# One wide matmul in place of two narrow ones in the output stage of a fused attention and mixture kernel

## The chip, the cores and the metric

The kernel runs on one core of one Trainium2 chip. The metric is the device time of the core in microseconds. A core has a matrix engine, TensorE (PE in the profile, its weight loads shown as PEld), the elementwise engines VectorE (DVE), ScalarE (ACT) and GpSimd (POOL), and DMA queues, here issued from SyncE (SP). PE writes its results to PSUM, which this kernel uses as eight banks of 128 x 512 words of 32 bits; ACT and DVE read them there, and POOL works on tiles in SBUF, the main on-chip memory. Each engine takes its instructions in the order in which the program has them, and waits on semaphores for the others.

## The reference, cut to what matters

```
kv  = einsum('bhsd,bhde->...')        # linear attention, 8 batches x 8 heads, 576 x 64
x   = rms-normalised q @ kv, scaled   # becomes 4608 tokens x 512
x   = P(h) / Q(h) @ w_out, h = x @ w_in           # 512 -> 2048 -> 512, P and Q polynomials
out = (silu(x @ w_gate) * (x @ w_val)) @ w_o2     # 512 -> 1536 -> 512
```

All is in float32. The part that counts here is the last product, a matrix g of 4608 x 1536 (the gated activations) times w_o2 of 1536 x 512.

## The kernel before, in words

The kernel goes through attention and the first mixture layer, then the gate and value products of the second layer, and ends with the output stage. Most matmuls take words of the type float32r (fp32r in the profile), and each of their operands is cut into a high and a low half by `split`: ACT copies the high half (line 95), and DVE or POOL subtracts it from the value to get the low half (line 98). A product of two such operands is three matmuls: high by high, high by low, low by high.

The output stage runs over 18 units: nine tiles of 512 tokens by two halves of 256 tokens (`units`, line 839). Each unit is one 2x2 block product in the Strassen-Winograd form, with seven products O_A11, O_A12, O_A22, O_S2, O_S1, O_S3 and O_S4 instead of eight. Each product (`o_product`, line 941) goes over the six slices of the inner dimension and does three matmuls for each (lines 946, 947, 948): the stationary operand is the half x of the activations, 128x128, loaded anew for each matmul, the moving one is 256 columns (HK) of the weights `wo`. One product fills half a PSUM bank, so a unit uses half of each of four banks; two sets of four banks alternate.

Other engines prepare and finish:

- `o_load` (SP) fetches g of a unit two units ahead. `o_sums_1` and `o_sums_2` (DVE, line 515, 128x768, tile graw) form the four sums of a unit. `o_split` makes the two halves of the operand of one product (ACT high, then DVE or POOL low, 128x768, tile xo). POOL makes those for A11 and A12, DVE the five others.
- Bank 0 collects three products one after the other. `o_snap` (ACT) copies it out after each: a after A11, b after S2, c after S3. PE may add the next product to the bank only after the copy.
- `o_merge` (DVE, line 515, tile sb) adds or subtracts another bank: a += bank 1; d = c - bank 2; c += bank 3; b += bank 3. Bank 3 first holds S1; after d and c are merged, S4 is added to it, and then it is merged into b. So PE's product S4 of a unit waits for that unit's merge c.
- `o_store` (SP) writes the unit out.

The order is written out by hand in `o_unit` (line 967). PE's order in unit v is A11, A12, S4 of unit v-1, A22, S2, S1, S3. DVE's is: merge d and merge c of unit v-1, splits S1 and S3, merge a, merge b of unit v-1, split S4, split A22 of unit v+1, four sums of unit v+1, split S2 of unit v+1. POOL's is split A11 of unit v+1, split A12 of unit v+1. In unit 1 its own split S2 stands behind the merges as well, since unit 0 does not make it. In unit 0 the products and merges of the last gate step are interleaved. The last unit (`o_last`, line 1011) has the order A11, S4 of unit 16, S2, S1, S3, S4, A22, A12, with the merges and three stores between. The weight halves `wo` are made in `o_halves` (line 889) from tiles tagged crg and crv, under the gate products.

Of the kernel before, what the change touches and what calls it, by code (L numbers as in the profile page):

```python
# [8 lines left out]
F32 = mybir.dt.float32  # L9
F32R = mybir.dt.float32r  # L10
# [3 lines left out]
ALU = mybir.AluOpType  # L14

P = 128
# [4 lines left out]
N = 512  # L21
# [20 lines left out]
def fused_kernel(ctx: ExitStack, tc: tile.TileContext, kv_main, kv_left, q_t, w_in, w_out, w_gate, w_val, w_o2, ab, g_norm, out):  # L42
# [13 lines left out]
    nc = tc.nc  # L56
# [16 lines left out]
    late = {}  # L73
# [20 lines left out]
    def act(out, in_, func=AF.Copy, **kw):  # L94
        nc.scalar.activation(out=out, in_=in_, func=func, **kw)  # L95

    def sub(eng, out, a, b):
        eng.tensor_tensor(out=out, in0=a, in1=b.bitcast(F32), op=ALU.subtract)  # L98
# [69 lines left out]
    for f in range(NF1):  # L168
        n = len(wa_src)
# [63 lines left out]
    for t in range(TILES):  # L233
        t0, ss = t * N, []
        while t0 < (t + 1) * N:
            b = t0 // S
            n = min((b + 1) * S, (t + 1) * N) - t0
# [276 lines left out]
    def tt(eng, out, a, b, op):  # L514
        eng.tensor_tensor(out=out, in0=a, in1=b, op=op)  # L515

    def halves_of(ap):
        return ap.rearrange("p (a n) -> p a n", a=2)


    HK = DM // 2
# [152 lines left out]
    steps = [(q, f) for q in range(1, len(seq)) for f in range(UP if q >= P2 else 0, NF2 if q >= P2 else UP)]  # L674
# [4 lines left out]
    def new_set(y):  # L679
        if y:  # L680
            return [ps_y.tile([P, N], F32, tag=f"y{m}", name="pb") for m in range(4)]
        b = [ps_a.tile([P, N], F32, tag=f"pa{m}", name="pb") for m in range(2)]
        return b + [ps_h.tile([P, N], F32, tag="ph", name="pb") for m in range(2)]

    def banks(i):
        if i not in bank:
            bank[i] = new_set(i % 2 == 0)
        return bank[i]
# [76 lines left out]
    def last_product(i):  # L765
        if i >= 0:
            product(i, 3, S_4, B_22, False)
# [62 lines left out]
    wo = {}  # L830
# [3 lines left out]
    o_x = {}  # L834
    o_sb = {}
# [3 lines left out]
    units = [(t, c) for t in order for c in range(2)]  # L839
    O_A11, O_A12, O_A22, O_S2, O_S1, O_S3, O_S4 = range(7)  # L840
    PRODUCTS = (V_11, V_21, V_T4, V_T2, V_T1, V_T3, V_22)
# [26 lines left out]
    def o_views(i):  # L868
        vals = [halves_of(w_views(raw_o[i, k])[2]) for k in range(2)]
        sums = [halves_of(raw_o[i, k].bitcast(F32).rearrange("p (n two) -> p n two", two=2)[:, :, 0]) for k in range(2)]  # L870
        return vals, sums
# [13 lines left out]
    def o_slot(k, shape, name):  # L885
        pool, tag = o_slots[k]
        return pool.tile(shape, F32R, tag=tag, name=name)

    def o_halves(i, part, eng):
        if part == 0:  # L890
            if i == UP - 1:
                wo[i] = [o_slot(7 + k, [P, 7, HK], "wo") for k in range(2)]
            else:
                u = late[f"u{i}"].tile([P, 2, 7, HK], F32R, tag=f"u{i}", name="wo")
                wo[i] = [u[:, k] for k in range(2)]
        vals, sums = o_views(i)
        src, at = ((vals[0][:, 0:1, :], slice(V_11, V_11 + 1)), (vals[1], slice(V_21, V_22 + 1)), (sums[0], slice(V_T1, V_T2 + 1)), (sums[1], slice(V_T3, V_T4 + 1)))[part]
        hi, lo = (w[:, at, :] for w in wo[i])
        act(hi, src)
        sub(eng, lo, src, hi)  # L900

    def o_load(v, k):
        if v < len(units):
            t, c = units[v]
            r = o_raw[v, k] = o_sum_to[v, k] = late["graw"].tile([P, UP, NH], F32, tag=f"g{k}", name="graw")
            nc.sync.dma_start(out=r, in_=g_dram[t, k][c])

    def o_part(v, k):
        a, b = T_OF[k]
        return (o_raw if k in (O_A11, O_A12, O_A22, O_A21) else o_sum_to)[v, a][:, :, b * P:b * P + P]  # L910
# [5 lines left out]
    def o_split(v, k, eng):  # L916
        if v < len(units):
            x = o_x[v, k] = o_slot(k, [P, 2, UP, P], "xo")
            r = o_part(v, k)
            act(x[:, 0], r)  # L920
            sub(eng, x[:, 1], r, x[:, 0])
# [8 lines left out]
    def o_sums_1(v):  # L930
        o_sum(v, O_S1, O_A21, O_A22, ALU.add)
        o_sum(v, O_S3, O_A11, O_A21, ALU.subtract)
# [2 lines left out]
        o_sum(v, O_S2, O_S1, O_A11, ALU.subtract)  # L935
        o_sum(v, O_S4, O_A12, O_S2, ALU.subtract)

    def o_banks(v):
        return [b[:, :HK] for b in banks(len(steps) + v)]

    def o_product(v, k, b, first=True):
        ps, x = o_banks(v)[b], o_x[v, k]
        for n, i in enumerate(I_ORDER):
            wh, wl = (w[:, PRODUCTS[k], :] for w in wo[i])
            start, stop = first and n == 0, n == UP - 1
            nc.tensor.matmul(ps, lhsT=x[:, 0, i, :], rhs=wh, start=start, stop=False, skip_group_check=not first)  # L946
            nc.tensor.matmul(ps, lhsT=x[:, 0, i, :], rhs=wl, start=False, stop=False, skip_group_check=not first)  # L947
            nc.tensor.matmul(ps, lhsT=x[:, 1, i, :], rhs=wh, start=False, stop=stop, skip_group_check=not first)  # L948

    def o_dst(v, name):  # L950
        row, col = {"a": (0, 0), "b": (0, HK), "d": (1, 0), "c": (1, HK)}[name]
        return o_sb[v][:, row, col:col + HK]

    def o_snap(v, name):
        if name == "a":
            o_sb[v] = late["p"].tile([P, 2, N], F32, tag="g", bufs=2, name="sb")
        act(o_dst(v, name), o_banks(v)[0])

    def o_merge(v, out, name, b, op=ALU.add):
        tt(nc.vector, o_dst(v, out), o_dst(v, name), o_banks(v)[b], op)  # L960

    def o_store(v, rows, cols=slice(0, N)):
        t, c = units[v]
        o = out[t * N + c * NH:t * N + c * NH + NH, :].rearrange("(m p) n -> p m n", p=P)
        nc.sync.dma_start(out=o[:, rows, cols], in_=o_sb[v][:, rows, cols])

    def o_unit(v):
        L = len(steps) - 1
        o_product(v, O_A11, 0)
        if v:  # L970
            o_merge(v - 1, "d", "c", 2, ALU.subtract)
            o_merge(v - 1, "c", "c", 3)
            if v == 1:
                o_split(v, O_S2, nc.vector)
        else:
            post(L, 0)
            o_split(v, O_S2, nc.vector)
        o_split(v, O_S1, nc.vector)
        o_split(v, O_S3, nc.vector)
        o_load(v + 2, 0)  # L980
        o_product(v, O_A12, 1)
        o_snap(v, "a")
        if v:
            o_product(v - 1, O_S4, 3, False)
        else:
            post(L, 2)
            post(L, 3)
            last_product(L)
        o_merge(v, "a", "a", 1)
        o_split(v + 1, O_A11, nc.gpsimd)  # L990
        if v:
            o_merge(v - 1, "b", "b", 3)
            o_store(v - 1, slice(0, 2))
        else:
            post(L, 4)
        o_product(v, O_A22, 2)
        o_split(v, O_S4, nc.vector)
        o_load(v + 2, 1)
        o_split(v + 1, O_A12, nc.gpsimd)
        o_product(v, O_S2, 0, False)  # L1000
        o_split(v + 1, O_A22, nc.vector)
        o_sums_1(v + 1)
        o_snap(v, "b")
        o_product(v, O_S1, 3)
        o_sums_2(v + 1)
        if v:
            o_split(v + 1, O_S2, nc.vector)
        o_product(v, O_S3, 0, False)
        o_snap(v, "c")

    def o_last(v):
        o_product(v, O_A11, 0)
        o_merge(v - 1, "d", "c", 2, ALU.subtract)
        o_merge(v - 1, "c", "c", 3)
        o_split(v, O_S1, nc.vector)
        o_split(v, O_S3, nc.vector)
        o_snap(v, "a")
        o_product(v - 1, O_S4, 3, False)
        o_product(v, O_S2, 0, False)
        o_snap(v, "b")  # L1020
        o_split(v, O_S4, nc.vector)
        o_merge(v - 1, "b", "b", 3)
        o_store(v - 1, slice(0, 2))
        o_product(v, O_S1, 3)
        o_merge(v, "b", "b", 3)
        o_product(v, O_S3, 0, False)
        o_snap(v, "c")
        o_product(v, O_S4, 1)
        o_merge(v, "b", "b", 1)
        o_store(v, slice(0, 1), slice(HK, N))  # L1030
        o_product(v, O_A22, 2)
        o_merge(v, "d", "c", 2, ALU.subtract)
        o_merge(v, "c", "c", 3)
        o_store(v, slice(1, 2))
        o_product(v, O_A12, 1)
        o_merge(v, "a", "a", 1)
        o_store(v, slice(0, 1), slice(0, HK))

    with tc.manual_schedule():
# [166 lines left out]
        for s in range(S1):  # L1206
            t, f = divmod(s, NF1)
# [61 lines left out]
            if t == TILES - 1:  # L1269
# [12 lines left out]
                elif 8 <= f < 12:  # L1282
                    k, c = divmod(f - 8, 2)
# [82 lines left out]
        for j in range(UP):  # L1366
            f, n = UP + j, 12 + 10 * j
# [19 lines left out]
        for n, i in enumerate(made):  # L1387
            at = (
# [3 lines left out]
            )[n % 3]  # L1392
# [37 lines left out]
        for v in range(len(units) - 1):  # L1430
            o_unit(v)
        o_last(len(units) - 1)


# [46 lines left out]
```

## Time and profile before

| | |
|---|---|
| time, median of 3 runs | 1680.99 us (1679.74 to 1682.69) |
| span of the profiled execution, first to last instruction | 1678.3 us (its own time is not listed) |
| PE busy | 1666.0 us, 99% of the span |
| PEld (weight loads) busy | 1415.8 us, 84% |
| DVE, ACT, POOL busy | 1371.2, 1073.6, 473.1 us |
| granted TensorE clock | 0.9 or more of full speed in all 40 slices, mean 1.000 |
| output stage | 1401.4 to 1674.9 us |

Busy PE is time in which at least one matmul runs; matmuls overlap, so the distance between the starts of two is what one costs. A group's mean is the duration of one instruction, waits for operands before it not counted. Rows of a timeline give the start, the duration (of all, where xN is over 1), the engine, the line, the tiles as out<-in with partitions x elements, and in brackets the idle time before and what ended it.

### The profile page before, as it was taken

The numbers are of one execution on the slowest core, as the hardware profiler recorded it, in microseconds if no ns is written. First come the engines' busy times: TensorE is split into PE (matmuls) and PEld (weight loads), VectorE is DVE, ScalarE is ACT, GpSimd is POOL, SyncE is SP. The second block draws the span as 40 slices with busy tenths as digits, with TensorE's granted clock in tenths as the row PEclk, the third lists the DMA queues.
The fourth block names the chain that finished last, engine by engine and source line by source line (L and its number), as shares of the span: only waits on it lengthen the run. The fifth ranks groups of instructions, "written<-read, shape, count | busy, mean of one in ns | idle before, by whom it ended". The sixth has DMA issues, their size and how long they took to land.

```text
span 1678.3 us, 24096 instructions
## 1 busy us (share of the span) xinstructions
PE 1666.0 (99%) x9040; PEld 1415.8 (84%) x9040; DVE 1371.2 (82%) x1913; ACT 1073.6 (64%) x1801; POOL 473.1 (28%) x331
## 2 busy tenths in 40 slices
PE   8999999999999999999999999999999999999999
PEld 5777888888888888888888888888888889999999
DVE  7999999999999999998996766778568859776665
ACT  7898888788788787877775444445435455444442
POOL 2112333333333343333330112223202155222221
PEclk9999999999999999999999999999999999999999
DMA  8861011011111110111425237243494354434431
GB/s 338 319 240 50 8 51 63 26 57 44 57 39 69 45 63 20 45 57 63 151 75 182 82 107 281 64 144 107 152 334 151 130 176 144 164 133 151 151 129 61
DMA packets 77850, 198.18 MB, mean 118 GB/s; under 512 B 6947, under 2 KB 35876, under 8 KB 75044
## 3 DMA queue, kind: packets, MB, share of 16 engines
q1 hardware_dynamic: 77732, 196.64, 33.3%
q8 instruction: 71, 1.16, 0.3%
q14 instruction: 47, 0.39, 0.1%
HBM read 130.02 MB, written 66.06 MB: 117 GB/s over the span
## 4 chain that ended last, share of the span: by engine, by line
PE 92%; DVE 4%; ACT 2%; DMA 2%; issue 1%; POOL 0%; SPq 0%; DVEq 0%; POOLq 0%; ACTq 0%
PE pb L112 10%; PE pb L113 10%; PE pb L114 10%; PE y L113 7%; PE ph L113 7%; PE ph L114 7%; PE ph L112 7%; PE y L114 7%; PE y L112 7%; PE pb L948 5%; PE pb L947 5%; PE pb L946 5%; DVE e L108 1%; ACT e L95 1%; DMA wraw<-in_w_in 1%
## 5 line engine op out<-in xcount | busy, mean ns | idle before, releaser
L98 POOL TENSOR_TENSOR ghl<-e,ghl 128x512 fp32r<-128x512 f32 x141 | 183.3, 1300 | 499.4 <-ACT ghl L95 289.8
L112 PE MATMUL pb<-xc,wu 128*128 128x512 f32 (+1 forms) x804 | 303.9, 378 | 0.0
L113 PE MATMUL pb<-xc,wu 128*128 128x512 f32 (+1 forms) x804 | 303.8, 378 | 0.0
L114 PE MATMUL pb<-xc,wu 128*128 128x512 f32 (+1 forms) x804 | 303.8, 378 | 0.0
L95 ACT ACTIVATE e<-pb 128x512 f32<-128x512 f32 (+1 forms) x162 | 92.8, 573 | 238.0 <-PE pb L114 237.7
L108 DVE SCALAR_TENSOR_TENSOR e<-e,e 128x512 f32<-128x512 f32 x285 | 226.3, 794 | 12.0 <-ACT e L95 4.9
L515 DVE TENSOR_TENSOR e<-e,pb 128x512 f32<-128x512 f32 (+1 forms) x216 | 140.6, 655 | 114.4 <-PE pb L114 63.5
L112 PE MATMUL ph<-x,wt 128*128 128x512 f32 x576 | 226.5, 393 | 0.3 <-ACT x L95 0.3
L113 PE MATMUL ph<-x,wt 128*128 128x512 f32 x576 | 225.0, 391 | 1.8 <-POOL x L98 1.6
L114 PE MATMUL ph<-x,wt 128*128 128x512 f32 x576 | 224.7, 390 | 0.0
L113 PE MATMUL y<-ghl,wt 128*128 128x512 f32 x564 | 221.5, 393 | 3.0 <-POOL ghl L98 2.8
L112 PE MATMUL y<-ghl,wt 128*128 128x512 f32 x564 | 221.5, 393 | 0.0
L114 PE MATMUL y<-ghl,wt 128*128 128x512 f32 x564 | 219.9, 390 | 0.0
L947 PE MATMUL pb<-wo,xo 128*128 128x256 f32 x756 | 213.9, 283 | 0.0
L948 PE MATMUL pb<-wo,xo 128*128 128x256 f32 x756 | 213.9, 283 | 0.0
L946 PE MATMUL pb<-wo,xo 128*128 128x256 f32 x756 | 213.9, 283 | 0.0
L112 PEld LDWEIGHTS pb<-xc,wu 128*128 128x128 f32 x804 | 151.0, 188 | 28.6 <-ACT e L95 0.4
L114 PEld LDWEIGHTS pb<-xc,wu 128*128 128x128 f32 x804 | 151.0, 188 | 28.1
L113 PEld LDWEIGHTS pb<-xc,wu 128*128 128x128 f32 x804 | 151.0, 188 | 28.0
L95 ACT ACTIVATE xo<-graw 128x768 fp32r<-128x768 f32 x122 | 99.1, 840 | 109.3 <-issue 49.9
L95 ACT ACTIVATE e<-ph 128x512 f32<-128x512 f32 x144 | 85.8, 596 | 119.3 <-PE ph L114 118.4
L946 PEld LDWEIGHTS pb<-wo,xo 128*128 128x128 f32 x756 | 145.1, 192 | 0.1
(138 smaller groups left out, 3409.2 us busy)
## 6 DMA issues: line engine op xcount, KB each, us to landing
graw<-gd SPq DMA_DIRECT2D x36, 768.0 KB, 4.4
gd<-gout SPq DMA_DIRECT2D x96, 256.0 KB, 2.2
kvm<-in_kv_main SPq DMA_DIRECT2D x32, 512.0 KB, 7.1
yraw<-yd SPq DMA_DIRECT2D x22, 512.0 KB, 7.0
q<-in_q_t SPq DMA_DIRECT2D x36, 256.0 KB, 3.7
yd<-sb SPq DMA_DIRECT2D x18, 512.0 KB, 3.5
out<-sb SPq DMA_DIRECT2D x17, 512.0 KB, 3.0
wraw<-in_w_in SPq DMA_DIRECT2D x16, 512.0 KB, 4.3
```

Source lines behind the costliest of these rows:

```text
L95: nc.scalar.activation(out=out, in_=in_, func=func, **kw)
L98: eng.tensor_tensor(out=out, in0=a, in1=b.bitcast(F32), op=ALU.subtract)
L108: nc.vector.scalar_tensor_tensor(out=out, in0=in0, scalar=scalar, in1=in1, op0=op0, op1=op1)
L112: nc.tensor.matmul(ps, lhsT=wh, rhs=xh, start=first, stop=False, skip_group_check=more)
L113: nc.tensor.matmul(ps, lhsT=wh, rhs=xl, start=False, stop=False, skip_group_check=more)
L114: nc.tensor.matmul(ps, lhsT=wl, rhs=xh, start=False, stop=last, skip_group_check=more)
L515: eng.tensor_tensor(out=out, in0=a, in1=b, op=op)
L946: nc.tensor.matmul(ps, lhsT=x[:, 0, i, :], rhs=wh, start=start, stop=False, skip_group_check=not first)
L947: nc.tensor.matmul(ps, lhsT=x[:, 0, i, :], rhs=wl, start=False, stop=False, skip_group_check=not first)
L948: nc.tensor.matmul(ps, lhsT=x[:, 1, i, :], rhs=wh, start=False, stop=stop, skip_group_check=not first)
```

## The change

In the 17 units before the last, the weight halves lie side by side (the high half's 256 columns, then the low half's), and the two matmuls whose stationary operand is the high half of x become one matmul of 512 columns. Its first 256 result columns hold high by high, the others high by low. The third matmul, low by high, is added to the second half of the bank. The bank is then 512 wide, and so are the snaps and merges, which write to a new tile `ob` (`o_both`, one for each row of the block, in the buffers tagged crg and crv). `o_fold` (POOL) adds the two halves at the end and writes sb; fold 1 stands behind merge c, fold 0 behind merge b, each ahead of POOL's next split in the program's order. The store then waits for the fold. The last unit keeps the three narrow matmuls. The weight tile changes its layout from [2, 7, 256] to [7, 2, 256], that of the last slice lies in two slots of four and three.

```diff
--- before.py
+++ after.py
@@ -889,13 +889,15 @@
     def o_halves(i, part, eng):
         if part == 0:
             if i == UP - 1:
-                wo[i] = [o_slot(7 + k, [P, 7, HK], "wo") for k in range(2)]
+                wo[i] = [o_slot(7 + k, [P, 4, 2, HK], "wo") for k in range(2)]
             else:
-                u = late[f"u{i}"].tile([P, 2, 7, HK], F32R, tag=f"u{i}", name="wo")
-                wo[i] = [u[:, k] for k in range(2)]
+                u = late[f"u{i}"].tile([P, 7, 2, HK], F32R, tag=f"u{i}", name="wo")
+                wo[i] = [u[:, 0:4], u[:, 4:7]]
         vals, sums = o_views(i)
         src, at = ((vals[0][:, 0:1, :], slice(V_11, V_11 + 1)), (vals[1], slice(V_21, V_22 + 1)), (sums[0], slice(V_T1, V_T2 + 1)), (sums[1], slice(V_T3, V_T4 + 1)))[part]
-        hi, lo = (w[:, at, :] for w in wo[i])
+        k = at.start // 4
+        w = wo[i][k][:, at.start - 4 * k:at.stop - 4 * k]
+        hi, lo = w[:, :, 0, :], w[:, :, 1, :]
         act(hi, src)
         sub(eng, lo, src, hi)
 
@@ -935,29 +937,46 @@
         o_sum(v, O_S2, O_S1, O_A11, ALU.subtract)
         o_sum(v, O_S4, O_A12, O_S2, ALU.subtract)
 
-    def o_banks(v):
-        return [b[:, :HK] for b in banks(len(steps) + v)]
+    def o_bank(v, b):
+        ps = banks(len(steps) + v)[b]
+        return ps if v < len(units) - 1 else ps[:, :HK]
 
     def o_product(v, k, b, first=True):
-        ps, x = o_banks(v)[b], o_x[v, k]
+        ps, x = o_bank(v, b), o_x[v, k]
         for n, i in enumerate(I_ORDER):
-            wh, wl = (w[:, PRODUCTS[k], :] for w in wo[i])
+            w = wo[i][PRODUCTS[k] // 4][:, PRODUCTS[k] % 4]
             start, stop = first and n == 0, n == UP - 1
-            nc.tensor.matmul(ps, lhsT=x[:, 0, i, :], rhs=wh, start=start, stop=False, skip_group_check=not first)
-            nc.tensor.matmul(ps, lhsT=x[:, 0, i, :], rhs=wl, start=False, stop=False, skip_group_check=not first)
-            nc.tensor.matmul(ps, lhsT=x[:, 1, i, :], rhs=wh, start=False, stop=stop, skip_group_check=not first)
+            if v < len(units) - 1:
+                nc.tensor.matmul(ps, lhsT=x[:, 0, i, :], rhs=w, start=start, stop=stop, skip_group_check=not first)
+                nc.tensor.matmul(ps[:, HK:], lhsT=x[:, 1, i, :], rhs=w[:, 0, :], start=False, stop=stop, skip_group_check=True)
+            else:
+                nc.tensor.matmul(ps, lhsT=x[:, 0, i, :], rhs=w[:, 0, :], start=start, stop=False, skip_group_check=not first)
+                nc.tensor.matmul(ps, lhsT=x[:, 0, i, :], rhs=w[:, 1, :], start=False, stop=False, skip_group_check=not first)
+                nc.tensor.matmul(ps, lhsT=x[:, 1, i, :], rhs=w[:, 0, :], start=False, stop=stop, skip_group_check=not first)
+
+    o_both = {}
 
     def o_dst(v, name):
-        row, col = {"a": (0, 0), "b": (0, HK), "d": (1, 0), "c": (1, HK)}[name]
-        return o_sb[v][:, row, col:col + HK]
+        row, col = {"a": (0, 0), "b": (0, 1), "d": (1, 0), "c": (1, 1)}[name]
+        if v == len(units) - 1:
+            return o_sb[v][:, row, col * HK:col * HK + HK]
+        if (v, row) not in o_both:
+            o_both[v, row] = late["p"].tile([P, 2, 2 * HK], F32, tag=("crg", "crv")[row], bufs=2, name="ob")
+        return o_both[v, row][:, col, :]
 
     def o_snap(v, name):
-        if name == "a":
+        if name == "a" and v == len(units) - 1:
             o_sb[v] = late["p"].tile([P, 2, N], F32, tag="g", bufs=2, name="sb")
-        act(o_dst(v, name), o_banks(v)[0])
+        act(o_dst(v, name), o_bank(v, 0))
 
     def o_merge(v, out, name, b, op=ALU.add):
-        tt(nc.vector, o_dst(v, out), o_dst(v, name), o_banks(v)[b], op)
+        tt(nc.vector, o_dst(v, out), o_dst(v, name), o_bank(v, b), op)
+
+    def o_fold(v, row):
+        if v not in o_sb:
+            o_sb[v] = late["p"].tile([P, 2, N], F32, tag="g", bufs=2, name="sb")
+        r = o_both[v, row].rearrange("p c (h n) -> p c h n", h=2)
+        tt(nc.gpsimd, halves_of(o_sb[v][:, row, :]), r[:, :, 0, :], r[:, :, 1, :], ALU.add)
 
     def o_store(v, rows, cols=slice(0, N)):
         t, c = units[v]
@@ -970,6 +989,7 @@
         if v:
             o_merge(v - 1, "d", "c", 2, ALU.subtract)
             o_merge(v - 1, "c", "c", 3)
+            o_fold(v - 1, 1)
             if v == 1:
                 o_split(v, O_S2, nc.vector)
         else:
@@ -990,6 +1010,7 @@
         o_split(v + 1, O_A11, nc.gpsimd)
         if v:
             o_merge(v - 1, "b", "b", 3)
+            o_fold(v - 1, 0)
             o_store(v - 1, slice(0, 2))
         else:
             post(L, 4)
@@ -1012,6 +1033,7 @@
         o_product(v, O_A11, 0)
         o_merge(v - 1, "d", "c", 2, ALU.subtract)
         o_merge(v - 1, "c", "c", 3)
+        o_fold(v - 1, 1)
         o_split(v, O_S1, nc.vector)
         o_split(v, O_S3, nc.vector)
         o_snap(v, "a")
@@ -1020,6 +1042,7 @@
         o_snap(v, "b")
         o_split(v, O_S4, nc.vector)
         o_merge(v - 1, "b", "b", 3)
+        o_fold(v - 1, 0)
         o_store(v - 1, slice(0, 2))
         o_product(v, O_S1, 3)
         o_merge(v, "b", "b", 3)
```

## Rows read from the trace of the kernel before

**Rows 1.** The page, chain that ended last by engine

```profile
PE 92%; DVE 4%; ACT 2%; DMA 2%; issue 1%; POOL 0%; SPq 0%; DVEq 0%; POOLq 0%; ACTq 0%
```

**Rows 2.** Stretches: the output stage, busy us of each engine (instructions), clock, DMA

```profile
1401.40:1674.90 273.50, 273.50 (x2275) 273.20 (x2273) 190.17 (x236) 118.58 (x181) 68.13 (x37) 1.00 0.39 135
```

**Rows 3.** PE in order of time, output stage: start, duration (us)

```profile
1439.82 0.28 PE L946 MATMUL pb<-wo,xo 128*128 128x256 f32 x1
...
1449.90 0.28 PE L946 MATMUL pb<-wo,xo 128*128 128x256 f32 x1
...
1674.78 0.28 PE L948 MATMUL pb<-wo,xo 128*128 128x256 f32 x1
```

**Rows 4.** PE in order of time, gate stage

```profile
1299.82 0.39 PE L114 MATMUL pb<-xc,wu 128*128 128x512 f32 x1
...
1301.86 0.39 PE L114 MATMUL pb<-xc,wu 128*128 128x512 f32 x1
```

**Rows 5.** DVE in order of time, units 1, 2, 9 and 10

```profile
1418.78 0.94 DVE L515 TENSOR_TENSOR sb<-sb,pb 128x256 f32<-128x256 f32 x2
...
1432.52 0.94 DVE L515 TENSOR_TENSOR sb<-sb,pb 128x256 f32<-128x256 f32 x2
1433.38 1.82 DVE L98 TENSOR_TENSOR xo<-graw,xo 128x768 fp32r<-128x768 f32 x2
...
1537.53 0.94 DVE L515 TENSOR_TENSOR sb<-sb,pb 128x256 f32<-128x256 f32 x2
1538.39 1.82 DVE L98 TENSOR_TENSOR xo<-graw,xo 128x768 fp32r<-128x768 f32 x2
1541.23 0.42 DVE L515 TENSOR_TENSOR sb<-sb,pb 128x256 f32<-128x256 f32 x1 [1.02 <-issue]
1543.34 0.42 DVE L515 TENSOR_TENSOR sb<-sb,pb 128x256 f32<-128x256 f32 x1 [1.68 <-PE pb L948]
...
1546.44 1.31 DVE L98 TENSOR_TENSOR xo<-graw,xo 128x768 fp32r<-128x768 f32 x1 [1.22 <-ACT xo L95]
1547.78 4.08 DVE L515 TENSOR_TENSOR graw<-graw 128x768 f32<-128x768 f32 x4
...
1552.65 0.94 DVE L515 TENSOR_TENSOR sb<-sb,pb 128x256 f32<-128x256 f32 x2
```

**Rows 6.** Groups of 1300 to 1678.3 us: count, busy us, mean ns, idle before

```profile
L515 DVE TENSOR_TENSOR sb<-sb,pb 128x256 f32<-128x256 f32 x73 | 30.4, 419 | 48.4 <-PE pb L948 31.6 <-issue 15.0
...
L95 ACT ACTIVATE sb<-pb 128x256 f32<-128x256 f32 x54 | 20.6, 382 | 39.5 <-PE pb L948 39.4
L95 ACT ACTIVATE e<-pb 128x512 f32<-128x512 f32 x32 | 19.1, 597 | 44.8 <-PE pb L114 44.8
```

**Rows 7.** Tile e on DVE: minimum, median, maximum in ns

```profile
L515 DVE TENSOR_TENSOR e<-e,pb x216: 415/686/691, 897.7 to 1408.6; 128x512 f32<-128x512 f32 x96, 128x256 f32<-128x256 f32 x12
```

**Rows 8.** Groups of POOL, whole span: count, busy us, mean ns, idle

```profile
L98 POOL TENSOR_TENSOR ghl<-e,ghl 128x512 fp32r<-128x512 f32 x141 | 183.3, 1300 | 499.4 <-ACT ghl L95 289.8 <-issue 130.3 <-PE y L114 40.4
...
L98 POOL TENSOR_TENSOR kvl<-kvc,kvh 64x256 fp32r<-64x256 f32 x10 | 10.0, 1004 | 2.2 <-ACT kvh L95 1.9
...
L98 POOL TENSOR_TENSOR wo<-wraw,wo 128x256 fp32r<-128x256 f32 x5 | 3.8, 757 | 18.9 <-ACT wo L95 18.9
```

**Rows 9.** Tile graw: minimum, median, maximum in ns

```profile
L98 DVE TENSOR_TENSOR xo<-graw,xo x86: 945/953/2610, 1398.7 to 1665.4; 128x768 fp32r<-128x768 f32 x86
L515 DVE TENSOR_TENSOR graw<-graw x68: 957/958/960, 1414.8 to 1656.7; 128x768 f32<-128x768 f32 x68
...
L98 POOL TENSOR_TENSOR xo<-graw,xo x36: 1838/1886/2468, 1395.9 to 1650.9; 128x768 fp32r<-128x768 f32 x36
```

**Rows 10.** POOL in order of time, units 2 and 9

```profile
1434.43 2.47 POOL L98 TENSOR_TENSOR xo<-graw,xo 128x768 fp32r<-128x768 f32 x1 [8.49 <-ACT xo L95]
...
1540.21 1.84 POOL L98 TENSOR_TENSOR xo<-graw,xo 128x768 fp32r<-128x768 f32 x1 [8.40 <-ACT xo L95]
1545.05 1.89 POOL L98 TENSOR_TENSOR xo<-graw,xo 128x768 fp32r<-128x768 f32 x1 [2.99 <-ACT xo L95]
```

## The prediction

> **What bounds the kernel now.** I read the page first: the chain that ended last is 92% PE [rows 1]. The stretches come next: in the output stage, 1401.4 to 1674.9 us, PE is busy for all 273.5 us, DVE for 190.2 and POOL for 68.1 [rows 2]. So PE alone sets this stage, and what slack the others have is to be counted inside a unit. PE's order in time gives its rate: 84 steps between matmuls of 256 columns take 10.08 us, 120 ns each, and 9 steps between matmuls of 512 columns take 2.04 us, 226.7 ns each [rows 3, 4]. At 2.4 GHz, the clock granted here (1.00 in rows 2), 256 columns are 106.7 ns and 512 are 213.3, so each matmul costs 13.3 ns beside its columns, however wide. A product (18 matmuls) takes 2.16 us and a unit of seven 15.12, which is also the distance between the merges of two units, 1537.53 and 1552.65 [rows 5]. Products are named as in the code; S4 of a unit stands third in the next one.
>
> The last matmul starts at 1674.78 [rows 3], so PE is through at 1674.90. The last stretch holds eight products (17.28 us) and began at 1657.62; unit 1, 16 periods earlier, began at 1415.70.
>
> **What the change takes from PE.** Two of the three matmuls of a step become one: 120+120 becomes 226.7, 13.3 ns less. 17 units x 7 products x 6 steps are 714 steps: 9.5 us, if PE stays the bound. A product is then 2.08 us and a unit 14.56. Should the narrow matmul, which adds to half of the bank that the wide one has just written, wait for it, up to the old 360 ns a step, the forecast below stays as it is, since PE is not its bound. The Trainium skill (TensorE: Matmul & The Clock Gate, Back-to-back issue gap) speaks against this part: an isolated matmul costs its columns plus 2.5 ns there, by which 714 joins would save an estimated 1.8 us. The rows show 13.3, so in this stream it does not hold.
>
> **What it adds.** Snaps and merges read 512 columns instead of 256. A snap on ACT goes from 382 to 597 ns [rows 6], a merge on DVE from 419 to 687 (the longest of its kind at 512 is 691) [rows 6, 7]. Three snaps and four merges a unit: ACT +0.6 us, DVE +1.07. Then two folds a unit on POOL, 128x512 out of two operands in SBUF, which the trace has not. POOL's other 128x512 subtractions take 1300 ns in the mean of 141 cases; the far end is 64x256 in runs of 64 elements, 1004 ns [rows 8], twice that by elements is 2.0 us. The fold reads runs of 256, so I take 1.30 and keep 2.0 as one end; the other is 0.76, the 128x256 row of the same group. The weight tile's new layout leaves number and size of the weight splits as they are, with halves in strided runs: nothing, hidden under the gate products that PE still runs then; a saving is excluded, no element goes, and uncovered it would be at most a blockage of 0.36 us (next paragraph) for each of 24 parts, 8.6 us. The store waits for the fold and holds up the g load behind it on SP by 3 to 4 us; that load is used most of a unit later, so nothing.
>
> **The price that decides: DVE and POOL exclude each other.** A split on DVE (two operands in SBUF) takes 953 ns, a sum 958, a split on POOL 1838 at least [rows 9]. But the DVE split of 1546.44 takes 1.31 [rows 5]; POOL's ran from 1545.05 to 1546.94 [rows 10]. 1546.44+1.31-0.95 is 1546.80: DVE worked only from 0.14 us before POOL's end. The other way round, POOL's split at 1434.43 takes 2.47 [rows 10], so it worked from 1435.06, 0.14 before the DVE pair of 1433.38 ended at 1435.20 [rows 5]. Who comes first keeps the other out. A merge, with one operand in PSUM, is not touched: 0.42 at 1541.23, inside POOL's 1540.21 to 1542.05 [rows 5, 10].
>
> So the folds cost DVE, though they run on POOL. I walk one unit of the changed kernel with these prices, in the order written for DVE. From rows 5: an independent DVE instruction starts 0.08 before its predecessor ends, the second merge of a pair 0.10 after the first, four sums take 4.08. Times in us from the start of merge d:
> merges d and c 0 to 1.48; split S1 1.40 to 2.35; fold 1 (asked at 1.55) works 2.22 to 3.52; split S3 (asked 2.27) 3.39 to 4.34; POOL's split A11 (asked 3.49) 4.21 to 6.05; merges a and b 4.26 to 5.56; split S4 (asked 5.48) 5.92 to 6.87; fold 0 6.74 to 8.04; split A22 (asked 6.79) 7.91 to 8.86; POOL's split A12 8.73 to 10.57; sums (asked 8.90) 10.44 to 14.52; split S2 14.44 to 15.39; the next merge d at 15.31.
> DVE has no idle time left, and PE's S4 cannot start before merge c has read its bank. The period is 15.31: PE alone wants 14.56 and took 15.12 before. That is +0.19 a unit, and PE now waits 0.75 us a unit ahead of S4. ACT's part fits: the high half for split S2 can be there at 14.4.
>
> **How the stage starts.** DVE is already late in unit 1: merge d of unit 0 starts at 1418.78, 3.1 us after that unit's last product, and the pair takes 0.94 [rows 5]; PE takes S4 of unit 0 at 1415.70+4.32 = 1420.02. Unit 0's own larger merge hides in a wait of its DVE chain for POOL, so I keep 1418.78. Merge c then ends at 1420.26, and S4 starts 0.3 late. Unit 1 has one split more (S2 of its own), between the merges and the folds: the same walk takes 17.4 us where before it was 13.74, to 1432.52 [rows 5]. Merge c of unit 1 ends at 1437.64; S4 of unit 1 starts at 1437.7, before at 1435.14.
>
> **Sum.** Up to S4 of unit 1: +2.6. Fifteen periods to S4 of unit 16: 15 x 0.19 = +2.8. In the last unit S4 stands second instead of third, by which only a stage that PE sets gets there sooner: +2.2. S4 itself is 0.1 shorter; the six products behind it are unchanged. Together +7.4: the span goes from 1678.3 to 1685.7. No own time is shown for the profiled execution; the median of the runs stands 2.7 above its span, and 1680.99+7.4 is **1688.4 us**.
>
> **Rivals.**
> 1. PE stays the bound (faster). For it: DVE is idle for 83 of 273 us [rows 2]. Against it: the walk, where none is left. The point is at 0.75 us a unit: a fold would have to take 0.92 instead of 1.30, or not keep DVE out. Then only the late start remains: S4 of unit 1 at 1435.1, fifteen units of 14.56 less 2.08 in the last one, 15.04 to the end: PE through at 1666.6 instead of 1674.9, -8.3 us, 1672.7.
> 2. In between (no change): hand-overs fall better, or a fold takes under 1.18, so that each of 16 units saves over 0.25: 15.06 or less, 1678 to 1684 us.
> 3. The folds are slow. Each 0.1 us costs 2 x 16 x 0.1 = 3.2 us: 1.6 us gives 1698, 2.0 gives 1711. For it the row of 1004 ns, against it the 141 plain ones [rows 8].
> 4. Each hand-over waits for the other's very end, without the 0.134 that the walk takes off: eight a unit are 1.07, seventeen us in all, 1705.5. Against it: 0.14 in both directions [rows 5, 10]. The Trainium skill (SBUF — State Buffer, Who interferes with whom) states the exclusion so, for the whole instruction and by who starts first. The trace agrees on who is kept out and not on the end.
>
> **Chances.** Forecast, DVE and POOL in turn at 15.06 to 15.85 a unit, 1684.4 to 1697: 0.67. Rival 1: 0.13. Rival 2: 0.13. Rivals 3 and 4: 0.07. Within 0.2%, about what can be told from no change, is 1677.6 to 1684.4: 0.13; faster 0.13, slower 0.74. The range leaves rivals 1, 3 and 4 out (0.20): 1677 to 1697.
>
> **What would show it.** In the changed profile DVE has no idle time between 1420 and 1660; splits S3, S4 and A22 and the first sum take 1.4 to 2.5 us; PE stands still for about 0.75 us ahead of each S4 until a DVE merge ends; like rows are 15.3 apart; folds read 1.3 to 2.1 us with the wait in them. I am wrong if like rows stand 14.56 apart and DVE idles, if a fold that nothing blocks takes far from 1.3, or if wide and narrow starts are not 226.7 and 120 ns apart.

## The result and the profile after

The changed kernel takes 1690.28 us in the median of 4 runs (1687.64 to 1692.06) against 1680.37 (1679.68 to 1682.69): ratio 1.0054, 95% interval 1.0037 to 1.0071. It is slower, as forecast, by 9.9 us instead of 7.4.

The page of the changed kernel first: the engines' busy time, then the chain.

```profile
span 1690.3 us, 22736 instructions
PE 1669.3 (99%) x8326; PEld 1381.3 (82%) x8326; DVE 1442.4 (85%) x1913; ACT 1081.7 (64%) x1801; POOL 558.8 (33%) x365
...
PE 7%; DVE 7%; ACT 1%; issue 1%; DVEq 0%; ACTq 0%
```

PE still shows 99% of the span, yet the chain is no longer PE alone: DVE has an equal share of what the page could follow back (it names only 16% of the span, so its shares are no measure here). The output stage, columns as in [rows 2]:

```profile
1404.70:1686.90 282.20, 273.96 (x1561) 236.88 (x1559) 260.17 (x236) 125.98 (x181) 153.78 (x71) 0.99 0.38 131
```

It lasts 282.2 us instead of 273.5. PE is idle for 8 us, and DVE is busy for 260 of 282, 70 us more than before although it has the same 236 instructions. POOL's time has more than doubled for 34 more. One unit shows why (start, duration); DVE first, then POOL.

```profile
1546.74 1.47 DVE L515 TENSOR_TENSOR ob<-ob,pb 128x512 f32<-128x512 f32 x2
1548.13 2.92 DVE L98 TENSOR_TENSOR xo<-graw,xo 128x768 fp32r<-128x768 f32 x2
1550.97 1.27 DVE L515 TENSOR_TENSOR ob<-ob,pb 128x512 f32<-128x512 f32 x2
1552.17 1.41 DVE L98 TENSOR_TENSOR xo<-graw,xo 128x768 fp32r<-128x768 f32 x1
1553.76 1.79 DVE L98 TENSOR_TENSOR xo<-graw,xo 128x768 fp32r<-128x768 f32 x1 [0.17 <-ACT xo L95]
1555.58 5.60 DVE L515 TENSOR_TENSOR graw<-graw 128x768 f32<-128x768 f32 x4
1561.10 0.95 DVE L98 TENSOR_TENSOR xo<-graw,xo 128x768 fp32r<-128x768 f32 x1
1561.97 1.47 DVE L515 TENSOR_TENSOR ob<-ob,pb 128x512 f32<-128x512 f32 x2
```

```profile
1548.29 1.94 POOL L515 TENSOR_TENSOR sb<-ob 128x512 f32<-128x512 f32 x1 [6.27 <-DVE ob L515]
1550.20 2.57 POOL L98 TENSOR_TENSOR xo<-graw,xo 128x768 fp32r<-128x768 f32 x1
1552.73 2.00 POOL L515 TENSOR_TENSOR sb<-ob 128x512 f32<-128x512 f32 x1
1554.69 2.55 POOL L98 TENSOR_TENSOR xo<-graw,xo 128x768 fp32r<-128x768 f32 x1
```

Against [rows 5, 10]: the period is 15.23 us (1546.74 to 1561.97), DVE's idle time has gone but for 0.17, the pair of splits has grown from 1.82 to 2.92 and the four sums from 4.08 to 5.60. POOL's split reads 2.55 instead of 1.84, as each side now waits for the other in turn. And PE, in order of time across the start of S4:

```profile
1547.51 0.28 PE L951 MATMUL pb<-wo,xo 128*128 128x256 f32 x1
1547.63 0.40 PE L950 MATMUL pb<-wo,xo 128*128 128x512 f32 x1
1547.87 0.28 PE L951 MATMUL pb<-wo,xo 128*128 128x256 f32 x1
1548.27 0.51 PE L950 MATMUL pb<-wo,xo 128*128 128x512 f32 x1
1548.61 0.28 PE L951 MATMUL pb<-wo,xo 128*128 128x256 f32 x1
1548.72 0.40 PE L950 MATMUL pb<-wo,xo 128*128 128x512 f32 x1
```

From narrow to wide it is 0.12 us elsewhere, but 0.40 from 1547.87 to 1548.27, where S4 waits for merge c, which ends at 1548.21. Before, PE's starts ran on at 0.12 there.

### The profile page after: what moved, and what is told of

It is laid out like the page before. It is cut to its first block, busy times and chain, and to the rows that moved or that the text cites. A ratio compares the mean times of both kernels' runs of the same rounds, so it can differ in the third digit from the quotient of the medians.

```text
span 1690.3 us, 22736 instructions
## 1 busy us (share of the span) xinstructions
PE 1669.3 (99%) x8326; PEld 1381.3 (82%) x8326; DVE 1442.4 (85%) x1913; ACT 1081.7 (64%) x1801; POOL 558.8 (33%) x365
## 5 line engine op out<-in xcount | busy, mean ns | idle before, releaser
L950 PE MATMUL pb<-wo,xo 128*128 128x512 f32 x714 | 255.6, 402 | 8.2 <-DVE ob L515 7.4
L951 PE MATMUL pb<-wo,xo 128*128 128x256 f32 x714 | 201.4, 282 | 0.0
L950 PEld LDWEIGHTS pb<-wo,xo 128*128 128x128 f32 x714 | 135.4, 190 | 44.9 <-DVE ob L515 12.6
L98 POOL TENSOR_TENSOR xc<-yraw,xc 128x1024 fp32r<-128x1024 f32 (+1 forms) x24 | 48.7, 2029 | 300.6 <-ACT xc L95 300.6
```

Of the source, the lines that this page charges most:

```text
L950: nc.tensor.matmul(ps, lhsT=x[:, 0, i, :], rhs=w, start=start, stop=stop, skip_group_check=not first)
L951: nc.tensor.matmul(ps[:, HK:], lhsT=x[:, 1, i, :], rhs=w[:, 0, :], start=False, stop=stop, skip_group_check=True)
```

## The experiments

Stage lengths are from the start of the first matmul of the stage to 0.12 us after the start of the last (273.5 before, 282.2 changed): the start of the stage differs from execution to execution by up to 6 us (last section). The ratio is to the kernel before.

| kernel | stage us | period us | ratio (95%) |
|---|---|---|---|
| no folds | 270.4 | 14.84 | 0.9977 (0.9966 to 0.9988) |
| folds on DVE | 272.0 | 14.84 | 0.9994 (0.9985 to 1.0004) |
| folds on DVE, grouped | 270.3 | 14.70 | 0.9989 (0.9979 to 0.9998) |
| before, plus folds on POOL | 274.7 | 15.12 | 1.0003 (0.9994 to 1.0012) |
| folds on DVE, grouped, S2 first | 270.8 | 14.70 | 0.9984 (0.9975 to 0.9993) |
| the same, snap a first | 269.1 | 14.70 | 0.9977 (0.9968 to 0.9986) |
| changed, S2 first | 280.3 | 15.2 | 1.0042 (1.0028 to 1.0056) |
| memsets for folds | 270.7 | 14.84 | one run |
| wide matmuls alone | 253.9 (mean clock 0.89) | 13.8 | one run |

**No folds.**

```
     def o_fold(v, row):
-        if v not in o_sb:
-            o_sb[v] = late["p"].tile([P, 2, N], F32, tag="g", bufs=2, name="sb")
-        r = o_both[v, row].rearrange("p c (h n) -> p c h n", h=2)
-        tt(nc.gpsimd, halves_of(o_sb[v][:, row, :]), r[:, :, 0, :], r[:, :, 1, :], ALU.add)
+        pass
     def o_store(v, rows, cols=slice(0, N)):
...
+        for row in range(2):
+            r = o_both[v, row].rearrange("p c (h n) -> p c h n", h=2)
+            nc.sync.dma_start(out=halves_of(o[:, row, :]), in_=r[:, :, 0, :])
```

> The change without the two folds: the store writes the first half of each bank alone, so the low-order terms are left out of the result. Theory (DVE and POOL keep each other out, the folds are the price): the period falls from 15.23 us a unit to the pace of PE, 6 steps of 353 ns by 7 products = 14.84, and the output stage to about 269.8 us (273.5 before, 282.2 with the change), so some 3 to 4 us faster than before. Rival A (the wide snaps and merges alone fill DVE): the period stays near 15.2. Rival B (PE itself is slower with the wide matmuls): at least 15.12.

Measured 270.4 us and 14.84 a unit, with wide matmuls, snaps and merges all in place: rivals A and B fall. DVE in one unit:

```profile
1542.05 1.47 DVE L515 TENSOR_TENSOR ob<-ob,pb 128x512 f32<-128x512 f32 x2
1543.44 1.82 DVE L98 TENSOR_TENSOR xo<-graw,xo 128x768 fp32r<-128x768 f32 x2
...
1547.58 0.69 DVE L515 TENSOR_TENSOR ob<-ob,pb 128x512 f32<-128x512 f32 x1 [1.38 <-PE pb L951]
...
1552.02 4.08 DVE L515 TENSOR_TENSOR graw<-graw 128x768 f32<-128x768 f32 x4
```

Splits and sums are back at 1.82 and 4.08, and DVE waits for PE again.

**Folds on DVE.**

```
-        tt(nc.gpsimd, halves_of(o_sb[v][:, row, :]), r[:, :, 0, :], r[:, :, 1, :], ALU.add)
+        tt(nc.vector, halves_of(o_sb[v][:, row, :]), r[:, :, 0, :], r[:, :, 1, :], ALU.add)
```

> The folds moved from POOL to DVE, each some 0.69 us of DVE's own time. Theory (a fold on POOL costs DVE 1.17 us or more by keeping it out, more than the fold itself costs on DVE): period 14.84, DVE with little idle time, stage about 271.3 us, about 2 us faster than before. Rival A (DVE has simply too much to do, on whatever engine the fold is): 1.4 us more on DVE, so the period goes up, above 15.3.

The same additions with 1.4 us more work for DVE make the stage 10 us shorter than on POOL (about 1.6 of them a stretch at half clock at the end of the changed kernel's stage, see below): 272.0, period 14.84. So DVE does not simply have too much to do; what a fold on POOL takes from DVE is more than what it costs on DVE: a unit of DVE with its folds took 15.23 us there and fits into 14.84 here. DVE's rows show both prices:

```profile
1538.03 1.47 DVE L515 TENSOR_TENSOR ob<-ob,pb 128x512 f32<-128x512 f32 x2
1539.54 0.69 DVE L515 TENSOR_TENSOR sb<-ob 128x512 f32<-128x512 f32 x1
1540.15 3.47 DVE L98 TENSOR_TENSOR xo<-graw,xo 128x768 fp32r<-128x768 f32 x2
...
1544.85 1.38 DVE L515 TENSOR_TENSOR sb<-ob 128x512 f32<-128x512 f32 x1
1546.15 1.81 DVE L98 TENSOR_TENSOR xo<-graw,xo 128x768 fp32r<-128x768 f32 x2
1548.00 4.08 DVE L515 TENSOR_TENSOR graw<-graw 128x768 f32<-128x768 f32 x4
```

A fold is 0.69 us here, 1.38 where POOL's split keeps it out, and the pair of splits still pays 1.65 for that of A11. Yet all of it fits into PE's period. Against the kernel before the time itself cannot be told from no change (0.9994).

**The kernel before, plus folds on POOL.**

```
+    def o_fold(v, row):
+        t = late["p"].tile([P, N], F32, tag=("crg", "crv")[row], bufs=2, name="ob")
+        r = halves_of(o_sb[v][:, row, :])
+        tt(nc.gpsimd, halves_of(t), r, r, ALU.add)
...
```

> The kernel before with two additions on POOL a unit that nobody uses, 128x512 out of SBUF, in the places of the folds; matmuls, snaps and merges stay narrow. Theory (exclusion): DVE's chain is then 15.23 less 4 x 0.266 = 14.2 us a unit, under PE's 15.12, so the middle of the stage stays at 15.12 and only unit 1, where DVE is late already, costs about 2 us: stage about 275.5; splits of DVE stretch to over 1.4 us all the same. Rival (folds on POOL slow the kernel by themselves, for instance through memory traffic): period above 15.12 throughout, some 8 us slower.

Stage 274.7 (275.5 expected), period 15.12 from unit 2 on, and 0.9 of the 1.1 us of cost lie in units 1 and 2, the rest in the last one. DVE's pair of splits stands at 2.67 behind the fold all the same:

```profile
1541.49 0.94 DVE L515 TENSOR_TENSOR sb<-sb,pb 128x256 f32<-128x256 f32 x2
1542.35 2.67 DVE L98 TENSOR_TENSOR xo<-graw,xo 128x768 fp32r<-128x768 f32 x2
...
1546.83 0.42 DVE L515 TENSOR_TENSOR sb<-sb,pb 128x256 f32<-128x256 f32 x1 [1.49 <-PE pb L948]
```

DVE still idles for 1.49 ahead of merge b. The price of a fold on POOL is paid out of slack as long as there is some. That the wider merges (1.07 us) had used it up in the changed kernel is argued from the expectation's sum and not shown by a run of its own. These additions are also cheaper than the folds: they read one tile twice and take 1.04 us where nothing blocks them, the folds 1.29.

**Memsets in place of folds.**

```
     def o_fold(v, row):
-        pass
+        for _ in range(2):
+            nc.gpsimd.memset(o_both[v, row], 0.0)
```

(on the kernel without folds.)

> In place of each fold POOL writes zeros twice over the merged tile, 2 x 0.95 us with no operand read, and the store takes that tile: the results of the first 17 units are left out. If every POOL instruction keeps DVE's two-operand ones out, whether it reads or not, 1.9 us in place of a fold's 1.3 must bring the period to 16.5 us and the stage to about 300. If only POOL instructions that read keep DVE out, the period is that of the kernel without folds, 14.84, and the stage about 270.5.

Stage 270.7, period 14.84: two memsets, longer than a fold, keep no split of DVE out. POOL's first row, and then DVE's pair of splits inside it and its split A22:

```profile
1538.29 1.97 POOL L977 MEMSET ob<- 128x1024 f32 x2 [7.25 <-DVE ob L515]
```

```profile
1538.15 1.82 DVE L98 TENSOR_TENSOR xo<-graw,xo 128x768 fp32r<-128x768 f32 x2
...
1544.43 2.29 DVE L98 TENSOR_TENSOR xo<-graw,xo 128x768 fp32r<-128x768 f32 x1 [1.17 <-ACT xo L95]
```

The pair of splits takes its plain 1.82 us while POOL writes from 1538.29 to 1540.26. So it is not any work of POOL that keeps DVE's two-operand instructions out: those that read two operands (folds, splits) do, one that only writes does not. The Trainium skill (SBUF — State Buffer, Who interferes with whom) has this limit, an instruction of GpSimd that only writes does not contend, and here the trace agrees. The memsets do cost DVE something in another way: they make POOL's splits later, so that the one from 1544.06 to 1545.90 meets DVE's split A22, which takes 2.29 us where it took 1.35 without folds. DVE is busy for 220.5 us instead of 208.4, and its slack pays.

**Grouped matmuls.**

```
+        if v < len(units) - 1:
+            for n, i in enumerate(I_ORDER):
+                w = wo[i][PRODUCTS[k] // 4][:, PRODUCTS[k] % 4]
+                nc.tensor.matmul(ps, lhsT=x[:, 0, i, :], rhs=w, start=first and n == 0, stop=n == UP - 1, skip_group_check=not first)
+            for n, i in enumerate(I_ORDER):
+                w = wo[i][PRODUCTS[k] // 4][:, PRODUCTS[k] % 4]
+                nc.tensor.matmul(ps[:, HK:], lhsT=x[:, 1, i, :], rhs=w[:, 0, :], start=False, stop=n == UP - 1, skip_group_check=True)
+            return
```

(with folds on DVE.)

> Folds on DVE, and within a product the six wide matmuls first and then the six narrow ones. In the changed kernel a wide and a narrow one in turn take 353 ns instead of the 346.7 of the prediction. Theory (it is the turn between widths that costs 6.6 ns): like steps are 226.7 and 120 ns, a product 2.08 us, the period 14.56, the stage about 267 us, 6 us faster than before. Rival (a wide matmul of these operands costs 233 ns by itself, for instance by its weight layout): 353 ns a pair as in the changed kernel, stage about 271.

Neither theory holds. PE, wide and narrow rows of one product and the start of the next:

```profile
1540.80 0.88 PE L952 MATMUL pb<-wo,xo 128*128 128x256 f32 x6
1541.52 1.55 PE L949 MATMUL pb<-wo,xo 128*128 128x512 f32 x6
1542.90 0.88 PE L952 MATMUL pb<-wo,xo 128*128 128x256 f32 x6
1543.62 0.63 PE L949 MATMUL pb<-wo,xo 128*128 128x512 f32 x2
```

Six wide take 1.38 us and six narrow 0.72, a product 2.10, the period 14.70. Within a product wide starts are 232 ns apart and narrow ones 119, in the mean of the stage. In turn they are 353 a pair without folds, grouped 350, by [rows 3, 4] 346.7.

The turn between widths is not by itself what costs the 6.6 ns, since the alternating pairs of the changed kernel run at two rates. Here are the first matmul of a product and that of the next, in two units:

```profile
1552.62 0.40 PE L950 MATMUL pb<-wo,xo 128*128 128x512 f32 x1
...
1554.74 0.40 PE L950 MATMUL pb<-wo,xo 128*128 128x512 f32 x1
...
1567.76 0.39 PE L950 MATMUL pb<-wo,xo 128*128 128x512 f32 x1
...
1569.84 0.39 PE L950 MATMUL pb<-wo,xo 128*128 128x512 f32 x1
```

Six pairs take 2.12 us in the first, 353 ns each, and 2.08 in the second, 347 each, as predicted. PE keeps one rate from one pause ahead of S4 to the next. Of the 112 products of units 1 to 16, 56 run at 353 and 29 at 347; the other 27 hold a pause, what follows it directly, or a stretch at half clock. What decides between the two rates stays open.

**Wide matmuls alone.**

```
-                nc.tensor.matmul(ps[:, HK:], lhsT=x[:, 1, i, :], rhs=w[:, 0, :], start=False, stop=stop, skip_group_check=True)
```

> The kernel without folds, and without the narrow matmul (low by high is left out too): only wide matmuls, six a product. If a wide matmul with these operands has the gate stage's cost, its starts are 226.7 ns apart, and the 232 of the grouped kernel came from its neighbours. If it is 232 here as well, the operands or the other engines' work make it so. DVE is then the bound in any case, as a product takes 1.4 us.

Their starts are 228 ns apart in the mean of 575, pauses and stretches at half clock left out; 226 or 227 in most. So the operands' layout is not it; that narrow ones follow in the same bank, or how dense the stream is, may be. As expected DVE is the bound: PE pauses in nearly every unit until a merge ends, and with the clock at half after most of these pauses (0.89 in the mean) the length of this stage is no measure of PE.

**S2 ahead of S4 in the last unit,** for the changed kernel and for the grouped one.

```
-        o_product(v - 1, O_S4, 3, False)
         o_product(v, O_S2, 0, False)
+        o_product(v - 1, O_S4, 3, False)
```

> The changed kernel, with nothing but S2 of the last unit ahead of S4 of unit 16. Theory (DVE and POOL set the time of merge c of unit 16, PE is late only for what stands behind it): the stage shortens by the one product that goes ahead, 2.16 us, and by what PE loses at half clock after its 2.7 us pause (10 starts at 0.43 us in the whole stage, about 1.7 us of it at its end): from 282.2 to about 278.4 us. Rival (PE's own rate is the bound): no change.

> Folds on DVE, wide matmuls grouped, and in the last unit the product S2 ahead of S4 of unit 16. The grouped kernel's PE waits 2.0 us for merge c of unit 16 ahead of that S4; a product of the last unit that needs nothing of it fills the wait. Theory: stage 270.3 less about 2 = 268.3 us, against 273.5 before: about 5 us faster than the kernel before, 1676. Rival (that wait is hidden behind DVE's chain to the last stores anyway): stage 270.3 as it was.

Both miss. The changed kernel gained 1.9 us, but about 1.6 of it are the stretch at half clock at its end, and 0.3 one in unit 2, which this execution did not have; next to nothing is left for the order. The grouped one lost 0.5: it gained 0.2 behind S4 of unit 1 and lost 0.7 ahead of it, where the edit changes nothing. In the changed kernel with S2 first, PE waits for another engine. The first row is PE's, the second shows ACT, which waits for the sums of DVE:

```profile
1666.35 0.39 PE L953 MATMUL pb<-wo,xo 128*128 128x256 f32 x1 [2.28 <-ACT sb L95]
```

```profile
1663.23 0.85 ACT L95 ACTIVATE xo<-graw 128x768 fp32r<-128x768 f32 x1 [4.83 <-DVE graw L515]
```

S2 adds to bank 0 and so needs snap a, which stands on ACT behind the high halves of S1 and S3, and these behind snap c of unit 16 and the high half of split S2, the row of 1663.23, which is held by DVE's sums. So a second way leads to the same late chain. The expectations had counted the wait that ended last and not the next one.

**The same with snap a ahead of the splits.**

```
+        o_snap(v, "a")
         o_split(v, O_S1, nc.vector)
         o_split(v, O_S3, nc.vector)
-        o_snap(v, "a")
```

> As the kernel with folds on DVE, grouped matmuls and S2 ahead of S4 in the last unit, and there snap a stands ahead of the splits S1 and S3 on ACT. In the run before, S2 waited 1.86 us for that snap, which stood behind both splits (1.57 us). Theory: S2 starts about 1.5 us earlier and the stage falls from 270.8 to about 269.2 us, 4.3 us under the kernel before, 1677 us. Rival (S4's merge is the later of the two): the wait only moves behind S2 and the stage stays above 270.4.

269.1 us as expected, ratio 0.9977 (0.9968 to 0.9986), 1677.8 us: this version is faster than both kernels, by 0.2% against the one before. That the size came out is partly luck. The starts around S2's pause were 1.86 us apart and are now 0.75, which is 1.1 us; the other 0.6 of the 1.7 lie ahead of S4 of unit 1 (34.4 us from the stage's start instead of 35.0), where the edit changes nothing. The stage:

```profile
1402.00:1671.20 269.20, 267.50 (x1561) 235.72 (x1559) 253.23 (x270) 126.14 (x181) 76.12 (x37) 1.00 0.41 137
```

## Why the prediction came out right, and where its sizes were off

- **The period.** Predicted 15.31, measured 15.23; the walk's parts are there one by one: sums of 5.60 (walked 5.62 from their asking at 8.90 to 14.52), merges of 0.68, most folds of 1.94 to 2.02 with the wait in them. The shortest fold of the stage, 1292 ns, bears out the 1.30:

```profile
L515 POOL TENSOR_TENSOR sb<-ob x34: 1292/1946/2024, 1424.0 to 1679.0; 128x512 f32<-128x512 f32 x34
```

- **The sum**, counted from the stage's first matmul (1401.37 before, 1404.68 changed). The first matmul of S4 of unit 1 and of S4 of unit 16, before and then changed:

```profile
1435.14 0.28 PE L946 MATMUL pb<-wo,xo 128*128 128x256 f32 x1
...
1659.78 0.28 PE L946 MATMUL pb<-wo,xo 128*128 128x256 f32 x1
```

```profile
1441.29 0.50 PE L950 MATMUL pb<-wo,xo 128*128 128x512 f32 x1 [2.48 <-DVE ob L515]
...
1670.16 0.50 PE L950 MATMUL pb<-wo,xo 128*128 128x512 f32 x1 [2.44 <-DVE ob L515]
```

To S4 of unit 1: +2.8 (predicted 2.6). Fifteen periods: +2.1 (2.8). The order in the last unit: +2.2 (2.2). From S4 of unit 16 to the end 16.7, where the prediction had 15.04 and the kernel before took 15.12: +1.6 (-0.1). Together 8.6 (7.4). The last is the term that was missed: PE had paused for 2.7 us there, and the clock granted afterwards was 0.58 in the mean, with up to 0.43 us from a wide start to the next narrow one instead of 0.24:

```profile
1670.10:1673.20 3.10, 3.04 (x11) 2.61 (x12) 2.83 (x3) 0.00 (x0) 1.92 (x1) 0.58 0.00 0
```

A like stretch follows the pause ahead of S4 of unit 1. From there to S4 of unit 2 it is 16.5 us; PE then runs at 14.84 a unit until it has caught DVE up, and about 0.3 us stay in the +2.1. Without the two stretches the sum would be some 6.7 us, an estimate; the changed kernel with S2 first had none in its stage and stands 6.8 above the kernel before. So the half clock more than makes up for periods that were forecast 0.08 too long, and that the total came so near is partly luck.

- **The rest of the profiled difference**, 3.3 us, is no work of the change: the stage starts at 1404.7 instead of 1401.4, and between 20 and 35 us, where the two programs are the same, the granted clock was 0.77 instead of 1.00 (last section). Two runs with a mean clock of 0.996 took 1691.9 and 1692.1 us, two with 0.999 took 1687.6 and 1688.7; the forecast of 1688.4 stands among the latter.
- **PE's part was over-sized.** Where PE sets the pace, in the version without folds, the join saves 6.7 ns a step and not 13.3, 4.8 us in 714 steps. The prediction added two costs measured each among its like, and by its own sign (starts not 226.7 and 120 ns apart) this part was wrong; in the changed kernel the sum of the two holds in some units and not in others. It did not show in the time, since PE was not the bound. After a unit at 347 a pair the starts ahead of S4 are about 0.7 us apart, near the 0.75 that was forecast as a pause, after one at 353 about 0.4. Rival 1, which the version without folds comes to, gives 270.4 and not 265.2; 4.2 of these 5.2 are fifteen units of 14.84 instead of 14.56.
- **Rival 4** (waits to the very end, 16.4 a unit) is refuted by the period, rival 3 by the 1292 ns. Moving the fold's engine, leaving the fold out and making POOL write alone each gave back the whole loss, so the exclusion is shown and not only argued.

## What to carry to other kernels

Before giving an addition to an idle POOL, ask what two-operand instructions DVE has at that time: here 1.3 us on POOL cost DVE more than the 0.7 us that the same addition takes on DVE itself. The share of busy time does not show it, as the waits are inside the durations; compare the longest duration of a group with its median, and walk one unit in the order of the queues. When a wait is to be filled, look for the next one behind it first.

## What was not expected of the hardware

PE's clock falls to half, the lower of its two levels, after some pauses and not after others; no run here shows what decides it. In the changed kernel pauses of 2.76 us (1438.5) and 2.72 us (1667.4) between starts were followed by 0.60 and 0.58; in the same kernel with S2 first a pause of the same 2.76 us was followed by 1.00. And the clock differs near the start of whole executions of the same code, the changed kernel first and then the kernel before:

```profile
20.00:35.00 15.00, 12.87 (x72) 8.10 (x71) 13.16 (x17) 10.54 (x20) 4.56 (x3) 0.77 0.96 372
```

```profile
20.00:35.00 15.00, 12.83 (x116) 8.89 (x116) 14.27 (x18) 13.19 (x24) 4.55 (x3) 1.00 0.99 388
```

PE did 72 matmuls in one and 116 in the other, and the 3 us are not made up later. The kernels without folds, with wide matmuls alone and before plus folds had it in their profiled executions too, the one with folds on DVE had not. So the spread of the runs, some 3 to 9 us, is larger than most effects here, and the length of the stage is the better measure.
